# Attention and a gated feed-forward layer on one core: whole steps of 512 columns in place of half steps in the first two blocks

## The chip, the core and the metric

The kernel runs on one core of a Trainium2 chip. The core has five engines with queues of their own, each of which works its instructions in the order in which they were issued: PE (TensorE, matrix products, results in the accumulator memory PSUM), DVE (VectorE) and ACT (ScalarE) for element-wise work, POOL (GpSimd, used for constants only) and SP (SyncE, which here issues all transfers). An engine whose next instruction waits for another engine does nothing else meanwhile. The metric is the device time of one execution in microseconds; the time before is the median of three runs.

## What is computed

A chunked local attention with eight memory keys per head, followed by a feed-forward layer of two products with a piecewise gate between them. Batch 4, 8 heads, 768 tokens, head size 64: 3072 tokens of width 512, hidden width 2048, all in 32-bit floats.

```python
for c in range(nc):                      # 24 chunks of 32 tokens
    l_start, r_end = max(0, c_start - 16), min(S, c_end + 8)
    k_full = np.concatenate([mem_k, k[:, :, l_start:r_end]], axis=2)
    v_full = np.concatenate([mem_v, v[:, :, l_start:r_end]], axis=2)
    scores = scale * np.matmul(q_c, k_full.transpose(0, 1, 3, 2))
    scores = scores - np.max(scores, axis=-1, keepdims=True)
    a = np.exp(scores)
    a = a / (np.sum(a, axis=-1, keepdims=True) + 1e-09)
    out[:, :, c_start:c_end] = np.matmul(a, v_full)
...
h = x @ w_in
g = np.where(h >= 1, h, np.where(h <= -1, 0.0, (h + 1) ** 2 / 4))
return g @ w_out
```

## The kernel before

The 3072 tokens are six blocks of 512 (`TB`), each of two halves of 256 (`HT`). The hidden width is 16 slices of 128 (`fc`). A **step** is one block and one slice: the hidden product (the slice of `w_in` against the block's x, giving 128 hidden values for the block's tokens), the gate, and the output product, which adds into four PSUM banks that hold the block's output until the slice 15 is in.

To keep the precision, x, weights and gate are each split into a high and a low part that PE takes, and each product is the sum of three: high by high, low by high, high by low. A whole step is so 12 hidden matmuls with 512 moving columns (tokens) and 12 output matmuls (four tiles of 128 tokens by three kinds) with 512 moving columns (output features). A half step is 12 hidden matmuls with 256 columns and 6 output matmuls with 512.

The gate of a step is three ACT operations (two Relu from PSUM into `gw` and `gt`, a Square), a sum on DVE (`gw`), a cast on ACT that makes the high part (`gh`), and a subtraction on DVE that makes the low part (`gl`). In the loop these are `gating`, `gate_sum`, `gate_high` and `gate_low` (lines 420 to 444), for half steps the same is written out in `half_step` (457 to 501).

The weights come as 64-bit words, 16 tensors of 1 MB, each with two slices. `decode` (153 to 173) makes them into high and low parts: a scaling on ACT, a shift and two combinations on DVE (`f`), a cast on ACT (`hi`, tile `wr`), a subtraction on DVE (`lo`, tile `wr`). All operations are 1024 columns wide. `weight_order` (614 to 619) says which slices come first: tensor 0 holds the hidden slices 0 and 1, tensor i the hidden slice i + 1 and the output slice i - 1.

The attention of block 0 is done in four pieces, g0 and g1 for its first half and g2 and g3 for its second (`first_attention`, 217 to 287), so that x of the first half is ready early. Each has 13 stages: scores on PE, maximum, subtraction, exponential (ACT), four operations of normalising on DVE, a transpose on PE, a copy on ACT, the values product on PE, and x's high (ACT) and low part (DVE). Those of the later halves, n0, n1 and so on (`attention`, 374 to 387), have transposes on DVE and 18 stages.

Up to the end of block 1 the order of issue is written out by hand, in the string `FIRST` (32 to 55). Each word there advances one chain by one stage, and everything that the stage has is issued at that place on the queue of its engine. `g` and `n` are attention pieces, `w` the decoding of a weight tensor, `+` the next load on SP's queue (the list `early`, 526 to 533). `A` and `B` are the half steps of block 0's first and second half, `C` and `D` those of block 1: `A7` is the first half with slice 7. A half step has six stages: hidden product; the three ACT operations; sum; high part; low part; output product. The last slice has two more, in which the results are copied and stored. Two consecutive half steps share one set of gate tiles. Hidden products use two PSUM banks in turn (`ps_h`); outputs have the four banks `a0` and `a1`; scores and values of the attention use the two banks `s`. The PSUM tiles of g0 to g3 lie in `s`, `a0` and `a1` (`PLACES`, 215).

From block 2 on a loop (570 to 605) issues whole steps: in each the hidden product of step s and the output product of step s - 2, with pieces of the next attention between. In its first two rounds, where there is no step s - 2 of its own, it finishes the last `LAST` = 4 half steps, two in a round.

Every operation is recorded through one helper, so the profile gives nearly all of them the line 68; they are told apart by tile: `ps_h` are hidden products, `ps_o` output products, `ps_s` scores, `ps_x` values, `f` and `wr` decoding, `gw`, `gt`, `gh` and `gl` gates, `xth` and `xtl` x, `mx`, `pr`, `den`, `rin` and `pt` attention, `ob` stored results.

Of the kernel before, what the change touches and what calls it, by code (L numbers as in the profile page):

```python
# [16 lines left out]
P = 128  # L17
CHUNK, LEFT, RIGHT = 32, 16, 8
TB = 512
# [18 lines left out]
    w10 + A4 B3 w5 B4 A5 w11 w6 + B4 w6 A4 w7 w7 B4 A5 B5 B4 w12 + A5 w6 B4 A5 B5 A5 w7 w13 A6 + B5  # L38
    w7 w8 A5 w8 B5 A6 B6 B5 w14 A6 w7 A6 B5 B6 A6 w8 w15 A7 B6 w8 w9 A6 w9 B6 A7 B6 B7 A7 w8 A7 B6
    B7 A7 w9 A8 B7 w9 w10 w10 A7 B7 A8 B7 B8 A8 w9 A8 B7 A8 B8 w10 A9 B8 w10 w11 w11 B8 A8 A9 B8 A9  # L40
    B9 w10 A9 A9 B8 w11 B9 B9 A10 w11 w12 w12 B9 A9 A10 B9 w11 B10 A10 w12 A10 B9 B10 A10 w12 w13
    A11 B10 w13 B10 A10 A11 B10 w12 n0 A11 w13 A11 B11 + n0 w13 B10 A11 B11 n0 A12 B11 n0 w13 B11
    A11 A12 n0 B12 n0 n0 B11 n0 B11 B12 A12 n0 A12 A13 A12 n0 n0 A12 A13 w14 n0 B13 w14 n0 A14 B13
    n0 B12 n0 w14 B12 B12 w14 A13 w15 B12 A13 + w14 n0 A13 A14 B14 w15 A13 n0 n0 B14 B13 n1 w15 B13
    B13 w15 A15 A14 + n1 A14 B13 A15 A14 w15 B15 n1 A14 B14 n1 A15 B14 n1 C0 A15 B15 n1 n1 B14 n1
    B14 C0 A15 n1 A15 n1 n1 C1 n1 n1 C2 C1 B15 n1 B15 C0 B15 n1 C0 A15 C2 C0 C1 A15 C2 C1 C2 B15 C1
    + n1 C2 n1 n1 C0 B15 D0 B15 C1 D0 D0 D1 D0 D0 C3 D1 D1 C2 D1 C3 D1 D0 C3 C3 C3 D2 D1 D2 D2 D3 D2
    D2 C4 D3 D3 C3 D3 C4 D3 D2 C4 C4 C4 D4 D3 D4 D4 D5 D4 D4 C5 D5 D5 C4 D5 C5 D5 D4 C5 C5 C5 D6 D5
    D6 D6 C6 D6 D6 D7 C6 C6 C5 D7 C6 D7 D6 C6 D7 D7 C7 n2 C7 C7 D8 C7 + n2 C6 n2 D8 D8 D7 n2 C7 D8
    n2 C8 D8 n2 n2 D9 C8 n2 C7 n2 D9 n2 n2 D8 C8 n2 C8 C9 D9 n2 D9 C8 D10 n2 C9 D9 C9 C8 D10 C9 D10  # L50
    D9 C9 D10 D10 n2 C10 + n2 n2 n2 D11 C10 C10 n3 D11 C10 D11 C10 C9 D11 + n3 D10 n3 C11 D11 n3 n3
    D12 C11 n3 n3 C10 n3 D12 n3 D11 n3 n3 C12 C11 n3 C11 D12 D13 C12 C11 n3 D12 n3 C11 D13 D12 C12
# [21 lines left out]
def attn_ffn_kernel(ctx: ExitStack, tc: tile.TileContext, first_qk, first_v, qk, vw, w, out):  # L74
# [380 lines left out]
    items = []  # L455

    def half_step(blk, half, fc):

        n = len(items)
        items.append((blk, half, fc))  # L460
        q = slice(half * HT, (half + 1) * HT)
        xh, xl = (x[:, :, q] for x in xts[blk])
# [33 lines left out]
        ob = apool.tile([P, 2, DM], F32, name="ob", tag="f", bufs=2)  # L496
        for t, copy in enumerate((dve.tensor_copy, act.copy)):
            copy(ob[:, t], acc[blk][2 * half + t])
            r0 = blk * TB + (2 * half + t) * P
            sp.dma_start(out[r0 : r0 + P, :], ob[:, t])  # L500
            yield
# [199 lines left out]
```

## Time and profile before

| | us |
|---|---|
| median of 3 runs (lowest, highest) | 614.69 (614.47, 614.77) |
| the profiled execution | 613.78 |
| its span, from the first to the last instruction | 612.0 |
| PE busy | 594.5 (97%), 5784 matmuls |
| DVE busy | 330.8 (54%) |
| ACT busy | 291.1 (48%) |
| moved by transfers | 55.36 MB |

The times of rows in the profile count from the span's start. In a row of the order of time, start and length in us come first, then the engine, the operation, what it writes and reads, shapes and the number of instructions merged; in brackets stands the idle time of the engine just before and what ended it. A matmul's recorded length has its way through the array in it, so that consecutive ones overlap: what one costs is read from start to start. "x" is a number of instructions. The granted clock of PE is a share of its full one.

### The profile page before, as it was taken

Reading aid. Unit: us, or ns where it says so; the run is one execution under the profiler, and the core shown is the slowest. Engines: PE = TensorE matmul, PEld = TensorE weight load, DVE = VectorE, ACT = ScalarE, POOL = GpSimd, SP = SyncE. Lnnn points to the kernel's source line nnn. Section 1 sums busy time; section 2 is a strip of 40 time slices with the busy share of each in tenths; the row PEclk is TensorE's granted clock in tenths of the full one; section 3 lists DMA queues with packets and bytes.
Section 4 is the critical chain, followed back from the end, with each engine's and each line's share of the span. In section 5 each row is a group of like instructions: output and inputs, shape, how many; then the busy total and the mean of one; then the engine's idle time right before and its main releaser. Section 6 shows DMA issues by size and latency. Waiting matters only on the chain.

```text
span 612.0 us, 12987 instructions
## 1 busy us (share of the span) xinstructions
PE 594.5 (97%) x5784; PEld 498.4 (81%) x5784; DVE 330.8 (54%) x514; ACT 291.1 (48%) x599; POOL 0.7 (0%) x6
## 2 busy tenths in 40 slices
PE   5799999999999999999999999999999999999996
PEld 3789998889988988888887888888888888888885
DVE  5899999983276734635523644722563632322222
ACT  3689865555444553444344343434443444433442
POOL 0000000000000000000000000000000000000000
PEclk8699999999999999999999999999999999999999
DMA  8999002422023213122201222100410000100001
GB/s 357 423 417 412 9 1 105 140 79 96 1 104 114 76 56 112 61 71 104 71 0 70 104 70 105 60 11 16 158 70 2 0 2 0 70 0 2 0 1 69
DMA packets 9848, 55.36 MB, mean 90 GB/s; under 512 B 1088, under 2 KB 1088, under 8 KB 5184
## 3 DMA queue, kind: packets, MB, share of 16 engines
q1 hardware_dynamic: 9792, 54.53, 23.4%
q8 instruction: 45, 0.74, 0.5%
q14 instruction: 11, 0.09, 0.0%
HBM read 48.23 MB, written 6.29 MB: 89 GB/s over the span
## 4 chain that ended last, share of the span: by engine, by line
PE 78%; DVE 18%; issue 2%; DMA 1%; ACT 1%; DVEq 0%; ACTq 0%
PE ps_o L68 37%; PE ps_h L68 36%; DVE f L68 7%; PE ps_x L68 3%; DVE wr L68 3%; PE ps_s L68 2%; DVE gw L68 2%; DVE pr L68 2%; DVE gl L68 1%; DVE pt L68 1%; DVE mx L68 1%; DVE den L68 1%; DMA qk<-in_first_qk_dram 1%; DVE xtl L68 0%; ACT pr L68 0%
## 5 line engine op out<-in xcount | busy, mean ns | idle before, releaser
L68 PE MATMUL ps_h<-xth,wr 128*128 128x256 f32 (+1 forms) x1024 | 202.9, 340 | 0.3 <-ACT xth L68 0.3
L68 PE MATMUL ps_o<-wr,gh 128*128 128x512 f32 x768 | 202.6, 395 | 0.5 <-DVE wr L68 0.5
L68 PEld LDWEIGHTS ps_h<-xth,wr 128*128 128x128 f32 x1024 | 164.4, 190 | 26.9 <-ACT xth L68 0.6
L68 PEld LDWEIGHTS ps_o<-wr,gh 128*128 128x128 f32 x768 | 141.3, 188 | 30.4 <-DVE wr L68 0.9
L68 DVE SCALAR_TENSOR_TENSOR gw<-gw,gt 128x256 f32<-128x256 f32 (+1 forms) x128 | 71.0, 556 | 167.3 <-ACT gw L68 166.5
L68 ACT ACTIVATE gw<-ps_h 128x256 f32<-128x256 f32 (+1 forms) x128 | 62.7, 490 | 161.2 <-PE ps_h L68 159.5
L68 PE MATMUL ps_o<-wr,gl 128*128 128x512 f32 x384 | 112.8, 395 | 0.2 <-DVE gl L68 0.2
L68 PE MATMUL ps_h<-xtl,wr 128*128 128x256 f32 (+1 forms) x512 | 110.4, 337 | 0.1
L68 DVE TENSOR_TENSOR gl<-gw,gh 128x256 fp32r<-128x256 f32 (+1 forms) x128 | 70.9, 555 | 66.5 <-ACT gh L68 65.7
L68 ACT CAST gh<-gw 128x256 fp32r<-128x256 f32 (+1 forms) x128 | 65.5, 514 | 65.3 <-DVE gw L68 65.2
L68 PEld LDWEIGHTS ps_h<-xtl,wr 128*128 128x128 f32 x512 | 83.6, 190 | 10.5 <-DVE xtl L68 0.3
L68 PEld LDWEIGHTS ps_o<-wr,gl 128*128 128x128 f32 x384 | 72.4, 189 | 17.5 <-DVE gl L68 0.6
L68 ACT ACTIVATE gw<-gw 128x256 f32<-128x256 f32 (+1 forms) x128 | 67.4, 526 | 0.0
L68 ACT ACTIVATE gt<-ps_h 128x256 f32<-128x256 f32 (+1 forms) x128 | 62.2, 486 | 0.0
L68 DVE STREAM_TRANSPOSE pt<-pr 32x512 f32<-32x512 f32 (+1 forms) x60 | 41.2, 698 | 1.3
L68 DVE SCALAR_TENSOR_TENSOR f<-w,f 128x1024 uint32<-128x1024 uint32 x32 | 39.1, 1221 | 0.4
L68 ACT ACTIVATE pr<-pr 128x1024 f32<-128x1024 f32 (+1 forms) x14 | 13.1, 937 | 41.0 <-DVE pr L68 41.0
L68 PEld LDWEIGHTS ps_x<-pt,v 64*64 64x64 f32 x1536 | 25.7, 142 | 5.8 <-issue 3.4
L68 PE MATMUL ps_x<-pt,v 64*64 64x32 f32 x1536 | 27.6, 226 | 1.5 <-DVE pt L68 0.9
L68 ACT CAST xth<-ps_x 128x512 fp32r<-128x512 f32 x24 | 13.0, 590 | 24.7 <-PE ps_x L68 24.7
L68 PEld LDWEIGHTS ps_s<-qk 64*32 64x32 f32 x1536 | 16.6, 108 | 8.2 <-issue 4.6
L68 PE MATMUL ps_s<-qk 64*32 64x64 f32 x1536 | 19.3, 232 | 3.6 <-issue 1.4
(27 smaller groups left out, 179.3 us busy)
## 6 DMA issues: line engine op xcount, KB each, us to landing
w<-in_w_dram SPq DMA_DIRECT2D x16, 1024.0 KB, 19.8
qk<-in_qk_dram SPq DMA_DIRECT2D x10, 1536.0 KB, 6.7
v<-in_vw_dram SPq DMA_DIRECT2D x10, 1024.0 KB, 4.9
out_dram<-ob SPq DMA_DIRECT2D x24, 256.0 KB, 2.0
qk<-in_first_qk_dram SPq DMA_DIRECT2D x4, 768.0 KB, 8.7
v<-in_first_v_dram SPq DMA_DIRECT2D x4, 512.0 KB, 12.8
```

Source lines behind the costliest of these rows:

```text
L68: return self.tc.keep_in_program_order(getattr(self.engine, name)(*args, **kwargs))
```

## The change

`half_step` becomes `early_step`, which takes the tiles of 128 tokens that it shall work on: two of them (256 tokens, as before) or all four (512). With four, the hidden product has 512 columns, the gate's operations are 512 wide and have their own set of tiles, and the output product has 12 matmuls. New letters stand for whole steps in the order of issue: `J` for block 0, `E` for block 1. Only the slices 0 to 3 of both blocks stay halves (A0 to A3, B0 to B3, C0 to C3, D0 to D3); J4 to J15 and E4 to E15 are whole. `FIRST` is a new list of 496 words instead of 638. The four half steps that the loop finished are now two whole ones (`LAST` = 2), which is the same work.

The new list also has another order in the parts that stay the same: g2's scores come before g1's and g0's values, the first two pieces of g2's softmax stand inside w0's decoding, three hidden products (A0, A1, A2) precede g3's transposes, n0's scores come between B2's hidden and A2's output product, n0's other stages are spread over w9 to w14.

```diff
-LAST = 4
+LAST = 2
...
-    def half_step(blk, half, fc):
-
-        n = len(items)
-        items.append((blk, half, fc))
-        q = slice(half * HT, (half + 1) * HT)
-        xh, xl = (x[:, :, q] for x in xts[blk])
-        hp = ps_h.tile([P, 512], F32, name="ps_h")[:, 0:HT]
+    items, halves = [], []
+
+    def early_step(name, blk, tokens, fc):
+
+        items.append(name)
+        size = len(tokens) * P
+        xh, xl = (x[:, :, tokens[0] * P : tokens[0] * P + size] for x in xts[blk])
+        n = 0
+        if size < TB:
+            n = len(halves) % 2
+            halves.append(name)
+        hp = ps_h.tile([P, 512], F32, name="ps_h")[:, 0:size]
...
-        g, t, gh, gl = (x[:, n % 2 * HT : (n % 2 + 1) * HT] for x in both["g"])
+        g, t, gh, gl = (x[:, n * HT : n * HT + size] for x in tiles)
...
-        pe_products(acc[blk][2 * half : 2 * half + 2], gh, gl, wh, wl, fc)
+        pe_products([acc[blk][t] for t in tokens], gh, gl, wh, wl, fc)
...
+    parts = {"A": (0, (0, 1)), "B": (0, (2, 3)), "J": (0, range(NT))}
+    parts |= {"C": (1, (0, 1)), "D": (1, (2, 3)), "E": (1, range(NT))}
...
-            for blk, half, fc in items[len(items) - LAST :][i * n : (i + 1) * n]:
-                for _ in chains[f"{'ABCD'[2 * blk + half]}{fc}"]:
+            for name in items[len(items) - LAST :][i * n : (i + 1) * n]:
+                for _ in chains[name]:
```

The two lists, up to the place where J4 begins and the matching place of the old one (line breaks of the file):

```diff
-    + + g0 g0 g0 + g0 g1 g0 + g0 g0 g1 g1 g0 g1 + g1 g0 w0 g1 g1 + g1 g0 w0 g1 w0 + g0 g1 w0 w0 g2 +
-    g0 w0 g1 w1 g2 + g2 g1 g0 g3 g2 + g1 g2 A0 + g3 g3 g2 g2 g3 g2 A1 A0 + g3 w2 g3 g3 g3 g2 w1 A1
-    w1 + g2 g3 w3 w1 g2 g3 A0 w1 g3 w2 + w2 g2 g3 A0 g2 w4 g3 A0 B0 w1 + w2 A0 B0 A1 w2 B0 B1 w3 +
-    B0 w2 A1 A2 B1 B0 A1 w3 A1 + A2 B1 w5 w3 B0 B1 A2 w3 + B1 B2 w4 A2 w3 w6 B1 A2 B2 + w4 A3 w7 B2
-    w4 B2 A2 A3 + B2 w5 w4 B3 A3 w5 w8 B2 A3 w4 + B3 A4 w9 A3 B3 w5 B3 A3 + A4 B3 w6 w5 A4 B4 w6 A4
+    + + g0 g0 + g0 g1 g0 + g0 g1 g1 g0 g0 + g1 g0 w0 g1 g0 + g1 g1 g1 g0 w0 g1 + w0 g2 g1 w0 g1 g2 +
+    w0 g2 w1 g0 w0 + g2 w1 g1 g2 + g0 g2 g2 g2 + g0 g2 w1 g3 g2 g1 w1 + A0 w2 g3 w1 g3 A1 w2 + g3 w1
+    w3 g3 g2 A0 g3 g3 + A1 g3 A2 w2 g2 w4 g3 g2 A2 A0 w2 g3 A0 + g3 w3 w2 A0 w3 A0 g3 g3 + w2 B0 A1
+    w3 A3 A1 B0 + A1 w3 B0 B1 w4 B0 w3 A3 A1 + B1 B0 w4 w5 B2 B1 w6 A2 w4 n0 + A2 B1 A2 w4 B1 A2 A3
+    w5 A3 B2 + A3 w5 B3 w8 B2 w7 B0 w4 + B2 w5 B3 A3 w9 B2 B3 B1 w6 B3 + w5 w6 J4 w10 B3 w5 + w6 w11
```

More of the change, by code (lines that the diff above doesn't have):

```diff
@@ L38 @@
[L38 to L52, printed above, removed]
@@ new lines @@
+    J12 n0 J13 w13 J12 J14 + n0 w14 n0 n0 w14 J12 w14 J14 J13 J14 w15 J14 n1 w15 w15 J15 + n1 w15
+    w15 J13 J15 n1 J15 n1 J14 C0 J15 n1 J14 n1 n1 C0 n1 n1 J15 C1 n1 n1 J15 n1 C1 n1 n1 C1 C0 C1 C2
+    J15 J15 C0 C1 n1 J15 J15 C0 C2 C2 C0 + n1 C2 n1 n1 C3 C2 C1 C3 C3 D0 C3 C3 C2 D0 D0 D1 D0 D0 n2
+    D1 D1 D2 D1 + n2 C3 D1 D2 n2 D0 D2 n2 D2 D3 n2 D2 D1 n2 n2 D3 n2 E4 D3 n2 D3 n2 n2 n2 D2 E4 D3
+    n2 E5 n2 E4 E4 E4 D3 E5 E6 E5 E5 E5 E4 E6 E6 E6 n2 E6 E7 + n2 n2 n2 n3 E7 E5 + n3 n3 E7 E8 n3 E7
@@ L468, in half_step @@
         yield
-        if n % 2 == 0:
-            both["g"] = (
+        if n == 0:
+            tiles = (
                 gpool.tile([P, TB], F32, name="gw", tag="gw"),
@@ L475, in half_step @@
             )
-        g, t, gh, gl = (x[:, n % 2 * HT : (n % 2 + 1) * HT] for x in both["g"])
+            if size < TB:
+                both["g"] = tiles
+        else:
+            tiles = both["g"]
+        g, t, gh, gl = (x[:, n * HT : n * HT + size] for x in tiles)
         act.activation(g, hp, AF.Relu, bias=0.5, scale=0.5)
@@ L488, in half_step @@
             acc.setdefault(blk, [None] * NT)
-            pair = two_banks(f"a{half}", "ps_o")
-            acc[blk][2 * half : 2 * half + 2] = [pair[:, t] for t in range(2)]
+            pair = two_banks(f"a{tokens[0] // 2}", "ps_o")
+            for t in tokens:
+                acc[blk][t] = pair[:, t % 2]
         wh, wl = weights(1, fc, 0), weights(1, fc, 1)
-        pe_products(acc[blk][2 * half : 2 * half + 2], gh, gl, wh, wl, fc)
+        pe_products([acc[blk][t] for t in tokens], gh, gl, wh, wl, fc)
         yield
@@ L495, in half_step @@
             return
[L496 to L500, printed above, removed]
+        for t in tokens:
+            if t % 2 == 0:
+                ob = apool.tile([P, 2, DM], F32, name="ob", tag="f", bufs=2)
+            (act.copy if t % 2 else dve.tensor_copy)(ob[:, t % 2], acc[blk][t])
+            r0 = blk * TB + t * P
+            sp.dma_start(out[r0 : r0 + P, :], ob[:, t % 2])
             yield
```

17 lines of the change are left out of this document (9 added, 8 removed).

## Prediction

> **What bounds the kernel now.** I read the page first, then six stretches of the trace cut where the PE's behaviour changes, then the order of time of PE, DVE and ACT inside them. The page's chain of work that ended last:
>
> ```profile
> PE 78%; DVE 18%; issue 2%; DMA 1%; ACT 1%; DVEq 0%; ACTq 0%
> ```
>
> The chain runs through DVE first and PE later. The table by stretch says where the hand-over is (columns: PE, PE weight load, DVE, ACT, POOL busy us with instruction counts, granted PE clock, DMA share, GB/s):
>
> ```profile
> 0.00:22.86 22.86, 13.72 (x400) 9.48 (x401) 14.03 (x24) 8.58 (x11) 0.70 (x6) 0.75 0.93 376
> 22.86:36.27 13.41, 11.18 (x180) 9.48 (x180) 12.99 (x21) 9.77 (x19) 0.00 (x0) 0.92 1.02 424
> 36.27:92.76 56.49, 56.49 (x361) 51.06 (x360) 56.28 (x85) 47.19 (x103) 0.00 (x0) 1.00 0.45 186
> 92.76:140.00 47.24, 45.74 (x751) 40.82 (x751) 43.49 (x71) 24.90 (x64) 0.00 (x0) 1.00 0.35 121
> 140.00:223.40 83.40, 83.40 (x1003) 75.58 (x1002) 43.73 (x85) 40.34 (x115) 0.00 (x0) 1.00 0.21 73
> 223.40:612.00 388.60, 383.94 (x3098) 312.00 (x3096) 160.27 (x232) 160.28 (x288) 0.00 (x0) 1.00 0.13 48
> ```
>
> From 36.27 us on PE is never idle except for 1.5 us between 92.76 and 140 (47.24 less 45.74) and the stores at the very end. DVE is just as full from 36.27 to 92.76 (56.28 of 56.49): decoding of weights, gates and the first attention all sit in its queue. So the first 140 us are a tie of two full engines, and from 140 us on it is PE alone (DVE busy 43.73 of 83.40). The issue list that the change rewrites ends at 223.40, where the loop's first whole step starts; all after that has the same instructions in both kernels. The end therefore moves by three things: the pure PE work of the list, PE time lost before the unbroken stretch, and PE gaps after it.
>
> **Part 1: PE work of whole steps.** The unbroken stretch 36.27 to 92.76 holds 360 matmuls: 20 half hidden products of 12 and 20 half output products of 6. That is 56.49 / 20 = 2.825 us for a half step, 5.65 for two halves. In the loop a whole step is read from two starts, three steps apart:
>
> ```profile
> 303.19 2.01 PE L68 MATMUL ps_h<-xth,wr 128*128 128x512 f32 x8
> 319.85 2.01 PE L68 MATMUL ps_h<-xth,wr 128*128 128x512 f32 x8
> ```
>
> 16.66 / 3 = 5.55 us. A pair of halves made into one whole step saves 5.65 - 5.55 = 0.096 us (24 matmuls of 256 columns become 12 of 512; the 12 output matmuls stay the same). The change makes whole steps of 12 pairs in each of two blocks: 24 x 0.096 = 2.3 us. In block 1 nothing else competes, so its half of this is safe. [...]
>
> **Part 2: relief of DVE and ACT.** The gates by both widths, and the decoding that shares their queues:
>
> ```profile
> L68 DVE TENSOR_TENSOR gl<-gw,gh 128x512 fp32r<-128x512 f32 x64 | 44.3, 693 | 60.1 <-ACT gh L68 60.1
> L68 DVE SCALAR_TENSOR_TENSOR gw<-gw,gt 128x512 f32<-128x512 f32 x64 | 44.2, 691 | 138.2 <-ACT gw L68 137.8
> L68 DVE SCALAR_TENSOR_TENSOR f<-w,f 128x1024 uint32<-128x1024 uint32 x32 | 39.1, 1221 | 0.4
> L68 ACT ACTIVATE gw<-gw 128x512 f32<-128x512 f32 x64 | 40.5, 632 | 0.0
> L68 ACT CAST gh<-gw 128x512 fp32r<-128x512 f32 x64 | 39.8, 622 | 41.7 <-DVE gw L68 41.7
> L68 ACT ACTIVATE gw<-ps_h 128x512 f32<-128x512 f32 x64 | 38.1, 595 | 127.7 <-PE ps_h L68 127.7
> L68 ACT ACTIVATE gt<-ps_h 128x512 f32<-128x512 f32 x64 | 37.9, 593 | 0.0
> L68 ACT ACTIVATE gw<-gw 128x256 f32<-128x256 f32 x64 | 26.9, 420 | 0.0
> L68 DVE SCALAR_TENSOR_TENSOR gw<-gw,gt 128x256 f32<-128x256 f32 x64 | 26.7, 422 | 29.1 <-ACT gw L68 28.6
> L68 DVE TENSOR_TENSOR gl<-gw,gh 128x256 fp32r<-128x256 f32 x64 | 26.5, 418 | 6.3 <-ACT gh L68 5.6
> L68 ACT CAST gh<-gw 128x256 fp32r<-128x256 f32 x64 | 25.6, 407 | 23.6 <-DVE gw L68 23.5
> L68 ACT ACTIVATE gw<-ps_h 128x256 f32<-128x256 f32 x64 | 24.6, 384 | 33.5 <-PE ps_h L68 31.9 <-DVE gl L68 1.3 <-issue 0.3
> L68 ACT ACTIVATE gt<-ps_h 128x256 f32<-128x256 f32 x64 | 24.3, 380 | 0.0
> L68 ACT ACTIVATE w<-w 128x1024 f32<-128x1024 f32 x16 | 18.8, 1176 | 0.0
> ```
>
> A whole step costs DVE 691 + 693 = 1.38 us against 2 x (422 + 418) = 1.68, so 0.30 less; ACT 595 + 593 + 632 + 622 = 2.44 against 2 x (384 + 380 + 420 + 407) = 3.18, so 0.74 less. For the 12 pairs of block 0 that is 3.6 us of DVE work out of a full queue, 8.9 of ACT. By itself this buys no time where PE is full too; it buys back PE's gaps where PE waited for DVE, which are these:
>
> ```profile
> 109.14 0.30 PE L68 MATMUL ps_x<-pt,v 64*64 64x32 f32 x4 [0.31 <-DVE pt L68]
> 109.88 1.94 PE L68 MATMUL ps_x<-pt,v 64*64 64x32 f32 x116 [0.43 <-DVE pt L68]
> 116.60 1.47 PE L68 MATMUL ps_s<-qk 64*32 64x64 f32 x128 [0.36 <-issue]
> 127.39 0.50 PE L68 MATMUL ps_o<-wr,gl 128*128 128x512 f32 x1 [0.20 <-DVE gl L68]
> 132.00 1.94 PE L68 MATMUL ps_x<-pt,v 64*64 64x32 f32 x116 [0.20 <-DVE pt L68]
> ```
>
> 0.31 + 0.43 + 0.36 + 0.20 + 0.20 = 1.5 us. Whether they go depends on the new order. For each list I added up the work queued on DVE up to the last transpose of an attention, and on PE up to the values product that reads it. DVE's work is counted by starts, which lie about 0.09 us closer than the durations (1.13 us for a 1024-wide operation, 0.60 for 512, 0.33 for 256); PE's by 1.43 and 1.39 us for the half products, 2.75 and 2.78 for the whole ones. For n0 DVE stands 8.9 us behind PE in the old list (96.6 against 87.7) and 7.8 in the new one (91.7 against 83.9); for n1 8.6 and 7.4. DVE comes 1.1 to 1.2 us earlier relative to PE. I take back 1.1 of the 1.5; the ends are 0 and 1.5.
>
> **Part 3: the start.** The rows that matter, DVE, then PE:
>
> ```profile
> 17.71 1.23 DVE L68 TENSOR_TENSOR wr<-f,wr 128x1024 fp32r<-128x1024 f32 x1 [1.17 <-ACT wr L68]
> 22.97 0.69 DVE L68 TENSOR_REDUCE mx<-ps_s 128x8 f32<-128x512 f32 x1 [0.92 <-PE ps_s L68]
> 37.50 1.22 DVE L68 TENSOR_TENSOR wr<-f,wr 128x1024 fp32r<-128x1024 f32 x1
> ```
> ```profile
> 22.86 2.07 PE L68 MATMUL ps_h<-xth,wr 128*128 128x256 f32 x8
> 24.73 0.77 PE L68 MATMUL ps_h<-xtl,wr 128*128 128x256 f32 x4
> 30.46 1.14 PE L68 MATMUL ps_x<-pt,v 64*64 64x32 f32 x64 [0.40 <-ACT pt L68]
> 36.27 1.11 PE L68 MATMUL ps_h<-xth,wr 128*128 128x256 f32 x8
> 37.69 1.12 PE L68 MATMUL ps_h<-xth,wr 128*128 128x256 f32 x8
> ```
>
> The old list makes DVE wait 1.17 us for ACT in w0's decoding and 0.92 for g3's scores. The new one puts g2's maximum and subtraction into the first wait and moves g3's behind w1's decoding, so both are filled. I count DVE's new queue from w0's last operation at 17.71 to w2's last one: eight 1024-wide operations (9.0 us), thirteen 512-wide (7.9), four small ones (0.8), two 256-wide (0.7): 18.5 us, so w2 is ready near 36.4 to 36.9 (the later end for operations that wait for the one before). In the old list it is ready at 37.50 + 1.14 = 38.6.
>
> PE's side: the new list queues hidden products of A0, A1, A2, then g3's transposes and values, A0's output, B0's hidden, and then A3's hidden, which needs w2. g3's values stand behind a long ACT queue: after g3's exponential (done near 27.2 by the same count) come, by starts that on ACT lie about 0.11 us closer than durations, two scalings of weights (1.05 each), three gates of three operations (0.85 each), g2's cast (0.5) and the copy itself (0.6), 5.8 us, so PE gets them near 33 and idles some 2.8 us before that. By 36.9 it has then done five half products. The old kernel has five at 37.69 (A0, A1, B0 hidden, A0 out, B1 hidden). Gain 0.8 us. Its ends: 2.2 us, if PE follows DVE's lead fully; and a loss of 1, if one of these hand-overs slips.
>
> The lead must hold afterwards. In the old list the furthest that a needed DVE result stands behind PE in these sums is 10.0 (A0's output), in the new one 11.3 (outputs of A2 and A3) and 11.2 (J4's output); DVE's head start of about 2 us pays for the 1.3. From J5 on no lag is over 10.2.
>
> **The rest, at nothing.** n0's scores move from behind B10 to behind B2's hidden: the same 1.5 us of PE, and the key buffer is free 50 us earlier, for a load that the idle DMA (0.45 and 0.35 of its time in these stretches) hides. SP's queue still issues the same 34 transfers, block 0's four stores among them. The two whole steps left to the loop hold what four halves held. Were any of this cover gone, one whole product would cost 2.75 us once.
>
> **Sum.** 2.3 + 1.1 + 0.8 = 4.2 us. The profiled execution took 613.78 us (span 612.0 and 1.78 around it), 0.91 under the median of 614.69; taken off the span the result is 607.8, off the profiled time 609.6, off the median 610.5, which is my number. A measurement here tells about 0.2% (1.2 us) from no change, so 613.5 and 615.9 bound "same".
>
> **Rivals.**
>
> *Only the pace arrives.* The lead at the start is lost in PE's new 2.8 us hole, and PE's gaps near 110 to 133 us move instead of closing. Against it stand the filled DVE waits. For it: the hole sits in front of work that starts at a low clock today; the eight matmuls at 22.86 take 1.87 us to the next row, where eight at the pace of the twelve from 36.27 to 37.69 take 0.95 (granted clock 0.75 in the first stretch, 0.92 in the second). If the hole brings that back, up to a dozen matmuls lose 0.11 us each, 1.3 us, more than the 0.8. [...] Time: 614.7 - 2.3 = 612.4.
>
> *DVE's queue blocks on whole gates.* Slower. A gate of 512 columns takes from PE's last product to its low part about 1.6 (ACT, three operations by starts) + 0.69 + 0.62 + 0.69 = 3.6 us, a half 0.85 + 0.42 + 0.41 + 0.42 = 2.1. DVE works its list strictly in order, so where a whole gate's sum or low part comes to the head of the queue before ACT has finished, the decoding behind it (w5 to w15) waits, and PE waits for the weights. The place is J4 to J15, 12 steps. DVE's relief pays for 0.30 us a step; beyond that PE slips. With w us of waiting a step the result is 614.7 - 2.3 - 0.8 + (12 w - 3.6), so it is slower than before from w = 0.56; at 0.75, half of the extra latency, it gives 617.0. Against it: DVE's waits from 36.27 to 140 in the old kernel are small though its list is as dense,
>
> ```profile
> DVE gw L68 <- ACT gw L68: 1.5, 1, 1.5
> DVE xtl L68 <- ACT xth L68: 0.5, 1, 0.5
> DVE den L68 <- ACT pr L68: 0.5, 1, 0.5
> DVE gl L68 <- ACT gh L68: 0.4, 1, 0.4
> ```
>
> and in the new list four other products, over 8 us of PE, stand between a whole step's hidden product and its output, against the gate's 3.6.
>
> *The change moves work but no end.* If block 0 stays bound by DVE and the new order loses at the start what block 1 gains (12 x 0.096 = 1.2 us), the time is 613.5 to 615.9, say 614.5.
>
> **Chances.** Forecast 0.55 (609.0 to 611.9); only the pace 0.23 (611.9 to 613.5); no end moved 0.10; blocked DVE 0.12. Faster 0.78, same 0.10, slower 0.12. The range leaves out the blocked case, some half of "same", and a small chance of all upper ends together (2.3 + 1.5 + 2.2 = 6.0): 608.7 to 614.3.
>
> **What would show it.** In the new profile: the list should end (first 512-wide hidden product after E15's) near 219 instead of 223.4; starts of whole steps 5.55 us apart from J6 on; DVE's waits at 17.7 and 23 gone and w2 ready near 36.5; a PE hole of about 3 us before g3's values near 33; PE idle under 0.5 us between 92 and 140. The forecast is wrong if DVE waits for ACT at the gates by over 0.3 us a step, if PE idles after 37 us, or if the granted clock falls near 33.

## The result and the profile after

The changed kernel takes 608.10 us (median of four runs, 607.99 to 608.29) against 614.58 for the old one (four runs, 613.84 to 614.77): a ratio of 0.9887, with a 95% interval of 0.986 to 0.9913. It is 6.5 us faster where 4.2 were forecast, and 0.6 us under the lower end of the forecast range. The profiled executions lie 5.6 us apart: 608.17 with a span of 606.4 after, against 613.78 and 612.0.

The page of the changed kernel, its chain of work that ended last:

```profile
PE 94%; DVE 3%; ACT 1%; DMA 1%; issue 0%; DVEq 0%; ACTq 0%
```

DVE carried 18% of this chain before and 3% now: after the start, nothing but PE sets the end. The table by stretch of the changed kernel, cut at the first hidden product, at the hidden product that needs w2 (36.77; its counterpart in the old kernel starts at 37.69, one half product behind the old table's cut at 36.27), at 92, at 140 and at the first whole step of block 2 (columns as before):

```profile
0.00:23.72 23.72, 14.56 (x404) 10.17 (x404) 16.60 (x30) 9.00 (x12) 0.70 (x6) 0.69 0.94 378
23.72:36.77 13.05, 11.47 (x192) 10.75 (x187) 12.91 (x20) 10.07 (x19) 0.00 (x0) 0.90 1.01 419
36.77:92.00 55.23, 55.23 (x386) 46.13 (x385) 54.87 (x70) 45.52 (x75) 0.00 (x0) 1.00 0.52 216
92.00:140.00 48.00, 47.98 (x641) 40.53 (x642) 41.92 (x61) 23.22 (x49) 0.00 (x0) 1.00 0.28 100
140.00:217.76 77.76, 77.76 (x801) 64.16 (x796) 39.14 (x58) 33.95 (x66) 0.00 (x0) 1.00 0.19 69
217.76:606.40 388.64, 383.99 (x3097) 312.00 (x3095) 160.12 (x231) 159.43 (x285) 0.00 (x0) 1.00 0.13 48
```

The list ends at 217.76 instead of 223.40, 5.64 us earlier, and the rest takes 388.64 instead of 388.60: the whole gain lies in the list, and none of it is given back later. Between 92 and 140 PE is idle for 0.02 us. From 36.77 on the granted clock is 1.00, and PE stops for nothing longer until the stores at the end.

The order of time on PE in the changed kernel, at the five places of the forecast:

```profile
21.59 1.08 PE L63 MATMUL ps_h<-ident,pr 128*128 128x128 f32 x4 [1.76 <-DVE pr L63]
22.61 1.19 PE L63 MATMUL ps_s<-qk 64*32 64x64 f32 x64
23.72 2.08 PE L63 MATMUL ps_h<-xth,wr 128*128 128x256 f32 x8
...
32.77 1.14 PE L63 MATMUL ps_x<-pt,v 64*64 64x32 f32 x64 [1.58 <-ACT pt L63]
...
36.77 1.12 PE L63 MATMUL ps_h<-xth,wr 128*128 128x256 f32 x8
...
103.85 2.07 PE L63 MATMUL ps_x<-pt,v 64*64 64x32 f32 x128
105.85 2.40 PE L63 MATMUL ps_h<-xth,wr 128*128 128x512 f32 x8
...
109.01 2.03 PE L63 MATMUL ps_o<-wr,gh 128*128 128x512 f32 x8
...
128.91 2.07 PE L63 MATMUL ps_x<-pt,v 64*64 64x32 f32 x128
130.91 1.19 PE L63 MATMUL ps_o<-wr,gh 128*128 128x512 f32 x4
...
195.55 2.01 PE L63 MATMUL ps_h<-xth,wr 128*128 128x512 f32 x8
...
201.10 2.01 PE L63 MATMUL ps_h<-xth,wr 128*128 128x512 f32 x8
```

Whole steps start 5.55 us apart (195.55 to 201.10). Products of the attention values, 128 small matmuls, take 2.00 us from start to start, both n0's (103.85 to 105.85) and n1's (128.91 to 130.91). The hole in front of g3's values is 1.58 us long and the clock stays up behind it (1.00 from 32.77 to 36.77). The same places in the old kernel, with what the prediction did not quote:

```profile
108.52 0.32 PE L68 MATMUL ps_x<-pt,v 64*64 64x32 f32 x8
...
111.75 1.20 PE L68 MATMUL ps_o<-wr,gh 128*128 128x512 f32 x4
...
125.17 1.09 PE L68 MATMUL ps_o<-wr,gh 128*128 128x512 f32 x4
...
128.42 1.11 PE L68 MATMUL ps_h<-xth,wr 128*128 128x256 f32 x8
...
131.38 0.42 PE L68 MATMUL ps_x<-pt,v 64*64 64x32 f32 x12
...
133.87 0.73 PE L68 MATMUL ps_o<-wr,gh 128*128 128x512 f32 x2
```

n0's values took 3.23 us there (108.52 to 111.75), n1's 2.49 (131.38 to 133.87): 1.23 and 0.49 more than now. The brackets of these products in the old trace show only 0.74 and 0.20 of idle time.

DVE's start in the changed kernel, and its waits between 37 and 140 us:

```profile
16.54 0.68 DVE L63 TENSOR_REDUCE mx<-ps_s 128x8 f32<-128x512 f32 x1
17.26 0.69 DVE L63 TENSOR_TENSOR pr<-ps_s,mx 128x512 f32<-128x512 f32 x1
17.87 1.22 DVE L63 TENSOR_TENSOR wr<-f,wr 128x1024 fp32r<-128x1024 f32 x1
...
35.54 1.21 DVE L63 TENSOR_TENSOR wr<-f,wr 128x1024 fp32r<-128x1024 f32 x1
```
```profile
DVE gw L63 <- ACT gw L63: 3.0, 3, 1.5
DVE gl L63 <- ACT gh L63: 0.9, 2, 0.5
```

The maximum and subtraction of g2 stand where DVE waited 1.17 us, w0's last operation starts at 17.87 with no wait, and w2's last one at 35.54 instead of 37.50. At the gates DVE waits 3.9 us in all, 0.33 a step if all of it is put on the 12 whole steps; this costs PE nothing, since PE is not idle there.

### The profile page after: what moved, and what is told of

It reads as the page before. It is cut to its first block, busy times and chain, and to the rows that moved or that the text cites. A ratio compares the mean times of both kernels' runs of the same rounds, so it can differ in the third digit from the quotient of the medians.

```text
span 606.4 us, 12265 instructions
## 1 busy us (share of the span) xinstructions
PE 591.0 (97%) x5496; PEld 483.7 (80%) x5496; DVE 325.6 (54%) x466; ACT 281.2 (46%) x503; POOL 0.7 (0%) x6
## 4 chain that ended last, share of the span: by engine, by line
PE 94%; DVE 3%; ACT 1%; DMA 1%; issue 0%; DVEq 0%; ACTq 0%
PE ps_o L63 44%; PE ps_h L63 44%; PE ps_x L63 3%; PE ps_s L63 3%; DVE f L63 1%; DMA qk<-in_first_qk_dram 1%; DVE pr L63 1%; DVE mx L63 0%; DVE den L63 0%; ACT w L63 0%; ACT gw L63 0%; DVE wr L63 0%; DVE xtl L63 0%; ACT pr L63 0%; ACT wr L63 0%
## 5 line engine op out<-in xcount | busy, mean ns | idle before, releaser
L63 PE MATMUL ps_h<-xth,wr 128*128 128x512 f32 (+1 forms) x832 | 197.3, 379 | 0.0
L63 PEld LDWEIGHTS ps_h<-xth,wr 128*128 128x128 f32 x832 | 148.7, 189 | 31.9 <-DVE wr L63 0.5
L63 DVE SCALAR_TENSOR_TENSOR gw<-gw,gt 128x512 f32<-128x512 f32 (+1 forms) x104 | 67.2, 648 | 170.0 <-ACT gw L63 169.5
L63 ACT ACTIVATE gw<-ps_h 128x512 f32<-128x512 f32 (+1 forms) x104 | 58.7, 564 | 167.8 <-PE ps_h L63 167.7
L63 PE MATMUL ps_h<-xtl,wr 128*128 128x512 f32 (+1 forms) x416 | 105.2, 375 | 0.0
L63 DVE TENSOR_TENSOR gl<-gw,gh 128x512 fp32r<-128x512 f32 (+1 forms) x104 | 67.4, 649 | 67.4 <-ACT gh L63 67.3
L63 ACT CAST gh<-gw 128x512 fp32r<-128x512 f32 (+1 forms) x104 | 61.1, 590 | 68.7 <-DVE gw L63 68.7
L63 ACT ACTIVATE gw<-gw 128x512 f32<-128x512 f32 (+1 forms) x104 | 62.5, 601 | 0.0
L63 ACT ACTIVATE gt<-ps_h 128x512 f32<-128x512 f32 (+1 forms) x104 | 58.2, 559 | 0.0
L63 ACT CAST wr<-f 128x1024 fp32r<-128x1024 f32 x16 | 16.8, 1050 | 9.3 <-DVE f L63 9.3
```

What stands on the lines that cost most here:

```text
L63: return self.tc.keep_in_program_order(getattr(self.engine, name)(*args, **kwargs))
```

## The experiments

The theory after the result: the 5.6 us are 2.3 of pace, 0.9 at the start and some 2.2 around n0 and n1. Its rivals: the last term comes from the order alone, or from the width's relief of DVE alone; or the start's part is not DVE's wait.

**e5: block 1 by halves again.** The changed kernel with each E written as C and D at the same place; block 0 as changed.

```diff
...
-    n2 E5 n2 E4 E4 E4 D3 E5 E6 E5 E5 E5 E4 E6 E6 E6 n2 E6 E7 + n2 n2 n2 n3 E7 E5 + n3 n3 E7 E8 n3 E7
+    D4 D3 n2 C5 D5 n2 C4 D4 C4 D4 C4 D4 D3 C5 D5 C6 D6 C5 D5 C5 D5 C5 D5 C4 D4 C6 D6 C6 D6 C6 D6 n2
...
-LAST = 2
+LAST = 4
```

> The new kernel with block 1's whole steps issued as two halves, one behind the other at the same places; start and block 0 as in the new kernel. The pace of 12 pairs, seen from the other side than in the run on block 1 with the old list. Theory (0.096 us a pair): 608.1 + 1.15 = 609.3. If PE stalls inside a run of matmuls without waiting for another engine, as it did for 1.1 us in block 1 of the run with halves at the new places, up to 1.4 more, 610.7. [...]

609.72 us (609.72 to 610.03), ratio to the old kernel 0.9914 (0.9889 to 0.994). Its span is 607.9, 1.5 over the changed kernel's. PE has a stop of 0.38 us at 29.07 that no engine causes, but this costs nothing: the hole before g3's values is 1.25 us instead of 1.58, and the product that needs w2 starts at 36.81 against 36.77. So the pace is best read inside block 1. From the first hidden product of slice 4 to the loop's first whole step it takes 70.97 us here (148.06 to 219.03) and 69.65 in the changed kernel (148.11 to 217.76): 1.3 us, or 0.11 a pair. By PE's last matmul (602.55 against 601.35) the difference is 1.2. The pace is confirmed by its size, and is if anything a little over the forecast's 0.096.

**e1: only block 1 whole, in the old order.** The old list, in which C and D from slice 4 on become E at the later of their two places.

```diff
-    D2 C4 D3 D3 C3 D3 C4 D3 D2 C4 C4 C4 D4 D3 D4 D4 D5 D4 D4 C5 D5 D5 C4 D5 C5 D5 D4 C5 C5 C5 D6 D5
+    D2 D3 D3 C3 D3 D3 D2 E4 D3 E4 E4 E4 E4 E5 E5 E4 E5 E5 E5 E6 E6 E6 E5 E6 E6 E7 n2 E7 E7 E7 + n2
...
-LAST = 4
+LAST = 2
```

> The old list of issue, only block 1's slices 4 to 15 as whole steps (each stage of a whole step stands where the later of its two halves stood); block 0 and the start are as before. It prices the pace alone, where nothing but PE is full. If a pair of halves costs 0.096 us more than a whole step (the theory): 12 x 0.096 = 1.15 us less, 613.4 against 614.6, and in the profile a span of 610.9 against 612.0. [...] If block 1 also lost time that the profile doesn't show as idle: 2 us or more.

614.98 us (614.13 to 615.58), ratio 1.0008 (1.0 to 1.0017): the expected 1.2 us did not appear. The merged list has a new gap on PE,

```profile
206.28 2.12 PE L66 MATMUL ps_o<-wr,gh 128*128 128x512 f32 x8 [1.38 <-ACT gh L66]
```

an output product placed too close behind its whole gate. Two more things in this profile have nothing to do with block 1. The stop of PE at the start is 1.67 us, where the old kernel's profile has 1.05 (below), and the row at 36.27 there starts at 37.12 here. And behind n0's values, whose idle pieces are those of the old kernel (0.33 and 0.43 us here, 0.31 and 0.43 there), the granted clock falls to 0.50:

```profile
112.62 1.81 PE L66 MATMUL ps_o<-wr,gh 128*128 128x512 f32 x4
117.09 1.08 PE L66 MATMUL ps_o<-wr,gh 128*128 128x512 f32 x4
```
```profile
114.00:116.00 2.00, 2.00 (x9) 1.72 (x8) 2.00 (x3) 1.51 (x5) 0.00 (x0) 0.50 0.86 311
```

Six outputs and a half hidden product take 4.47 us from start to start here; the same work took 2.93 in the old kernel (111.75 to 114.68). PE so comes to n1's scores 2.0 us later (118.57 against 116.60), and the outputs around n1 lose nothing any more (1.48 us for the six, 2.79 for the twelve), although DVE's work up to there is unchanged: a later PE closes these gaps as well. As a measure of the pace this run is inconclusive; its new gap shows that a whole gate without room in front of its output product costs as much as the pace gives in block 1.

**e3: the new order, all steps by halves.** The changed list with each J and E split into its two halves in place.

```diff
...
-    B2 w7 J4 w7 J5 + w6 w7 w12 w6 + w7 B3 J4 J5 w8 J6 w7 + J4 J5 w13 J4 w9 J5 J4 J6 w9 + J5 w15 J6
+    w11 B2 w7 A4 B4 w7 A5 B5 + w6 w7 w12 w6 + w7 B3 A4 B4 A5 B5 w8 A6 B6 w7 + A4 B4 A5 B5 w13 A4 B4
...
-LAST = 2
+LAST = 4
```

> The new list with every whole step issued as its two halves, one right after the other at the same places: order without width. Theory: the start gains 0.9 us as in the new kernel, the pace nothing, and with 0.30 us more DVE work a step the gaps at n0 and n1 are back: 614.6 - 0.9 = 613.7. Rival (the order closes the gaps): 614.6 - 0.9 - 2.0 = 611.7.

612.77 us (612.45 to 613.11), ratio 0.9973 (0.9962 to 0.9983), between the two expectations. Its span of 610.7 has a stop of PE of 1.10 us at 172.67 that no engine causes; 609.6 without it. PE's waits from 92 to 140 are one:

```profile
PE ps_h L68 <- DVE wr L68: 0.7, 1, 0.7
```

So the new order by itself closes most of the gaps. n0's values take 2.00 us (104.87 to 106.87) and n1's 1.99 (130.70 to 132.69), as in the changed kernel. What is left stands behind n0's values, where PE waits for weights:

```profile
106.87 0.73 PE L68 MATMUL ps_h<-xth,wr 128*128 128x256 f32 x4
109.31 1.12 PE L68 MATMUL ps_h<-xth,wr 128*128 128x256 f32 x8
```

This half hidden product takes 2.44 us where an undisturbed one takes 1.43, and some 0.1 more goes in the outputs behind it: 1.1 us lost in all. The old kernel lost 2.7 around n0 and n1 and the changed one loses 0.5 (both counted below), so the order brings 1.6 and the width 0.6. The spans agree: old 612.0, less 0.9 for the start is 611.1; e3's 609.6 leaves 1.5 to the order; the further 3.2 down to 606.4 are 2.3 to 2.6 of pace and 0.6 to 0.9 of width. This split rests on single profiles, and by the spans on taking the stop off.

**e2: whole steps in the old order.** Both blocks merged as in e1.

```diff
...
-    w10 + A4 B3 w5 B4 A5 w11 w6 + B4 w6 A4 w7 w7 B4 A5 B5 B4 w12 + A5 w6 B4 A5 B5 A5 w7 w13 A6 + B5
+    J4 w11 w6 + J4 w6 w7 w7 J4 J5 J4 w12 + w6 J4 J5 w7 w13 + J5 w7 w8 w8 J5 J6 J5 w14 w7 J5 J6 w8
...
-LAST = 4
+LAST = 2
```

> The old list in both blocks, whole steps for the slices 4 to 15 (each stage where the later of its halves stood). Width without the new order. Theory: the pace gives 2.3 us, and DVE's relief of 0.30 us a step closes the gaps of PE around n0 and n1 (about 2 us lost there by starts, 1.5 of it idle); the start is unchanged: 614.6 - 4.3 = 610.3. Rival: the gaps are closed by the new places of n0 and n1, not by width; then the pace alone is left, 612.3, and the gaps near 110 to 133 us are still in the profile. Second rival: stages set at the later place come too late and open new gaps; then over 612.3.

623.63 us (617.95 to 623.97), ratio 1.0129 (1.01 to 1.0158): slower than either expectation, by the mechanism of the second rival, new gaps. The order of time on PE at n0's values, and the table by stretch behind it:

```profile
109.00 0.30 PE L63 MATMUL ps_x<-pt,v 64*64 64x32 f32 x4 [1.68 <-DVE pt L63]
109.74 2.71 PE L63 MATMUL ps_x<-pt,v 64*64 64x32 f32 x116 [0.43 <-DVE pt L63]
112.39 3.78 PE L63 MATMUL ps_o<-wr,gh 128*128 128x512 f32 x8
```
```profile
106.00:112.00 6.00, 3.72 (x127) 3.03 (x127) 5.84 (x8) 2.64 (x5) 0.00 (x0) 0.88 0.01 3
112.00:117.00 5.00, 5.00 (x27) 3.97 (x22) 5.00 (x8) 1.59 (x3) 0.00 (x0) 0.50 0.61 210
```

PE reaches n0's values before DVE has their transposes, 2.3 us of idle time in pieces; then the granted clock falls to 0.50, and eight output matmuls take 3.78 us where the changed kernel's take 2.03. At a second place PE stops for 2.53 us without a releaser (at 201.75), and eight output matmuls behind it take 3.17, the clock being 0.50 again from 203 to 206. The executions of this run differ by 6 us (617.95 to 623.97), and the profile is of the longest. The run changes two things at once, the width and, by the rule of the later place, where each stage stands. It shows that whole steps merged so into the old order cost more than they give; it does not price the width's relief alone.

**e10: the new order with DVE's relief taken back.** The changed kernel with one 256-wide operation more on DVE in each whole gate of block 0 (12 x 0.33 = 4.0 us).

```diff
         dve.scalar_tensor_tensor(g, g, 1.0, t, op0=ALU.min, op1=ALU.add)
+        if blk == 0 and size == TB:
+            dve.tensor_tensor(spare, spare, spare, op=ALU.subtract)
...
+    spare = const.tile([P, HT], F32, name="spare")
+    pool.memset(spare, 0.0)
```

> The new kernel with one more DVE operation of 256 columns before each gate's low part in the 12 whole steps of block 0 (0.33 us each by starts, 4.0 us in all: what two half gates would cost more than a whole one). Width's relief of DVE taken back, pace and order kept. If the relief is what closed the gaps around n0 and n1: up to 2 us, 610. If the order closed them: DVE waits 4.4 us between 37 and 140 in the new kernel, which take the work up, and the time is 608.1 to 608.6.

612.97 us (611.84 to 613.52), ratio 0.9961 (0.9943 to 0.9979), 4.9 us slower than the changed kernel and well past what either expected. PE at the same place, and its stretch:

```profile
104.72 1.94 PE L63 MATMUL ps_x<-pt,v 64*64 64x32 f32 x116 [0.43 <-DVE pt L63]
107.05 2.07 PE L63 MATMUL ps_h<-xth,wr 128*128 128x512 f32 x4 [0.40 <-ACT wr L63]
110.12 2.08 PE L63 MATMUL ps_h<-xth,wr 128*128 128x512 f32 x4 [1.00 <-DVE wr L63]
```
```profile
108.00:112.00 4.00, 3.00 (x8) 1.84 (x7) 4.00 (x5) 1.25 (x4) 0.00 (x0) 0.50 0.65 252
```

1.8 us of idle time: n0's values break up again (0.43), and the larger waits are for the weights of the hidden product behind them (0.40 and 1.00). And again a clock of 0.50: this hidden product takes 5.6 us without its 1.00 of waiting (107.05 to 113.69), where the changed kernel's takes 3.2 (105.85 to 109.01). So about half of the 4.9 us is the clock. n1's values take 2.00 us (133.57 to 135.57), with PE 4.7 us later there than in the changed kernel.

What this run takes back is also more than what the width gives. By starts, as the prediction counts DVE's queue, the operations of two half gates take 4 x 0.33 = 1.32 us and those of a whole one 2 x 0.60 = 1.20: a relief of 0.12 us a step, 1.4 in the 12 steps, against the 4.0 put back here. So the run shows how little room DVE has at n0 even in the new order; it does not show that the relief of 1.4 us was needed. For that e3 is the measure: without width 1.1 us are lost there, with it 0.5.

**e6 and e9: less work for DVE in the old kernel.** The third operation of decoding is left out for the tensors 5 to 9 (e6) and 5 to 15 (e9, with `if i < 5`): these weights lose their signs.

```diff
-        dve.scalar_tensor_tensor(f, u, 0x80000000, f, op0=ALU.bitwise_and, op1=ALU.bitwise_or)
+        if i not in range(5, 10):
+            dve.scalar_tensor_tensor(f, u, 0x80000000, f, op0=ALU.bitwise_and, op1=ALU.bitwise_or)
```

> The kernel before, with the decoding of the tensors 5 to 9 shortened by its third DVE operation (the signs of these weights are left out): 5 x 1.13 = 5.7 us less work in DVE's queue between 50 and 90 us, everything else as before. If DVE's full queue makes the gaps of PE around n0 and n1: the lost 2 us between 92 and 140 go, 614.5 - 2.0 = 612.5, and the stretch before 92 does not change, because PE is full there. If the gaps come from the places of n0 and n1 in PE's queue or from accumulator banks: 614.5.

> The kernel before, with the third DVE operation of the decoding left out for all tensors from 5 to 15 (the signs of these weights are left out): 11 x 1.13 = 12.4 us less in DVE's queue, 7 of it while n0 and n1 are worked on. With five tensors n0's loss went from 1.23 to 0.35 us and n1's (1.5 us in three places) stayed. If n1's losses are DVE's load too: PE's lost time between 92 and 140 us falls from 2.4 to about 1.1, what the new kernel has there, and the time to 612.0. If they come from n1's place (13.4 us of PE products between its scores and its values for a softmax chain of nearly that length; 15.4 in the new list): they stay, 613.2.

e6: 613.32 us (612.86 to 613.97), ratio 0.9975 (0.9962 to 0.9989). e9: 612.76 (612.08 to 616.51), ratio 0.9959 (0.9935 to 0.9982). Both lie between their expectations. PE at n0's values, first in e6, then in e9:

```profile
108.63 2.42 PE L68 MATMUL ps_x<-pt,v 64*64 64x32 f32 x128
110.98 1.19 PE L68 MATMUL ps_o<-wr,gh 128*128 128x512 f32 x4
```
```profile
109.33 2.26 PE L68 MATMUL ps_x<-pt,v 64*64 64x32 f32 x128
111.52 1.21 PE L68 MATMUL ps_o<-wr,gh 128*128 128x512 f32 x4
```

From start to start 2.35 and 2.19 us, where the old kernel has 3.23 and the changed one 2.00: DVE's load was the cause at n0. The six outputs before n1's scores take 1.94 us in e6 (113.89 to 115.83; 1.92 in the old kernel) and 1.49 in e9 (114.44 to 115.93), which also lightens DVE's later decoding: this loss was DVE's load too. The idle piece there has no releaser in the profile, but a row of DVE explains it. In the old kernel

```profile
115.21 1.28 DVE L68 TENSOR_TENSOR xtl<-ps_x,xth 128x512 fp32r<-128x512 f32 x2
```

is the last read of n0's values out of the banks `s`, into which n1's scores go. It ends at 116.49, and the scores start at 116.60; in e6 the pair is 115.72 and 115.83. The twelve outputs take 3.25 us in e6 as in the old kernel and 2.80 in e9. n1's values stay slow in both: 2.47 us in e6 and 2.39 in e9 (130.26 to 132.65), so this part, 0.4 us, is not shown to be DVE's load. In all the losses around n0 and n1 are 1.8 us in e6 and 0.7 in e9, of the old kernel's 2.7. e9's profile is of an execution of 615.04 us, over the run's median: it has a stop of 2.27 us at 196.75, behind the places read here.

**e4: the wait at the start put back.** The changed kernel with g2's maximum and subtraction behind w0's last operation.

```diff
-    + + g0 g0 + g0 g1 g0 + g0 g1 g1 g0 g0 + g1 g0 w0 g1 g0 + g1 g1 g1 g0 w0 g1 + w0 g2 g1 w0 g1 g2 +
-    w0 g2 w1 g0 w0 + g2 w1 g1 g2 + g0 g2 g2 g2 + g0 g2 w1 g3 g2 g1 w1 + A0 w2 g3 w1 g3 A1 w2 + g3 w1
+    + + g0 g0 + g0 g1 g0 + g0 g1 g1 g0 g0 + g1 g0 w0 g1 g0 + g1 g1 g1 g0 w0 g1 + w0 g2 g1 w0 g1 + w0
+    w1 g0 w0 g2 g2 + g2 w1 g1 g2 + g0 g2 g2 g2 + g0 g2 w1 g3 g2 g1 w1 + A0 w2 g3 w1 g3 A1 w2 + g3 w1
```

> The new kernel with g2's maximum and subtraction put back behind w0's last DVE operation, so that DVE waits for ACT in w0's decoding again (1.17 us before). One change of order in the start, undone. Theory: DVE's queue sets the start, so w2 and the first unbroken stretch of PE come 1.0 to 1.2 us later, and the time is 609.2 against 608.1. Rival: the hole of 1.6 us that PE has before g3's values takes the delay up, and the time stays at 608.1.

609.52 us (609.29 to 609.6), ratio 0.9919 (0.9906 to 0.9932), as the theory had it. DVE's row, then the product on PE that needs w2:

```profile
17.48 1.22 DVE L63 TENSOR_TENSOR wr<-f,wr 128x1024 fp32r<-128x1024 f32 x1 [1.17 <-ACT wr L63]
```
```profile
37.80 1.12 PE L63 MATMUL ps_h<-xth,wr 128*128 128x256 f32 x8
```

The 1.17 us of waiting are back, the product moves from 36.77 to 37.80, and the span from 606.4 to 607.5. Here a wait in DVE's full queue is passed on to the end.

**e7: the same wait filled in the old kernel.**

```diff
-    + + g0 g0 g0 + g0 g1 g0 + g0 g0 g1 g1 g0 g1 + g1 g0 w0 g1 g1 + g1 g0 w0 g1 w0 + g0 g1 w0 w0 g2 +
-    g0 w0 g1 w1 g2 + g2 g1 g0 g3 g2 + g1 g2 A0 + g3 g3 g2 g2 g3 g2 A1 A0 + g3 w2 g3 g3 g3 g2 w1 A1
+    + + g0 g0 g0 + g0 g1 g0 + g0 g0 g1 g1 g0 g1 + g1 g0 w0 g1 g1 + g1 g0 w0 g1 g2 w0 + g0 g1 w0 g2
+    g2 w0 + g0 w0 g1 w1 + g1 g0 g3 g2 + g1 g2 A0 + g3 g3 g2 g2 g3 g2 A1 A0 + g3 w2 g3 g3 g3 g2 w1 A1
```

> The old list with one change in the start: g2's scores move ahead of g0's values and g2's maximum and subtraction into DVE's first wait, before w0's last operation, as in the new list; g3's maximum stays where it was. If the filled wait is what the start gained by: 614.5 - 1.2 = 613.3. Rival: PE stops inside g3's scores, at its 350th matmul, in every run of the old start (1.05 to 2.03 us, no other engine awaited) and never in the new one; if that stop comes from the supply of instructions, g3's scores end at the same 23 us, DVE waits longer for them, and the time stays within 0.4 of 614.5.

614.72 us (613.85 to 618.01), ratio 1.0003 (0.9985 to 1.0021): no gain; the rival's number. PE in the scores of g3:

```profile
19.94 0.45 PE L68 MATMUL ps_s<-qk 64*32 64x64 f32 x13
22.05 1.06 PE L68 MATMUL ps_s<-qk 64*32 64x64 f32 x51 [1.66 <-issue]
```

The 0.88 us for which PE waited for DVE there (0.45 us of scores started at 20.36 in the old kernel) are gone, but PE then stops for 1.66 us in the middle of one product with nothing to wait for; the old kernel stops there for 1.05. DVE, which needs these scores, waits 1.17 us for them instead. So in the old order filling DVE's wait alone gains nothing: the stop, 0.6 us longer here, takes it up.

**e11: the stop moved.** The stop comes at PE's 350th matmul. In the old kernel the 8 warming matmuls of 512 columns become 68 of 60 columns, so that every later instruction of PE stands 60 places further back in the stream.

```diff
-            pe.matmul(ps, warm[:, 0:P], warm, start=True, stop=True)
+            pe.matmul(ps[:, 0:60], warm[:, 0:P], warm[:, 0:60], start=True, stop=True)
...
-    keep_warm(8)
+    keep_warm(68)
```

> The kernel before, with its 8 warming matmuls of 512 columns made 68 of 60 columns (about the same time): every later matmul stands 60 places further in PE's stream. If PE's stop of 1.05 to 2.03 us at its 350th matmul comes from the supply of instructions, it stays near the 350th and so moves out of g3's scores into g1's values product; if it has to do with g3's scores themselves, it stays at their 14th matmul, now the 410th. The time is not forecast to a microsecond: 614.5, within 1.5.

The stop is again at the 350th matmul, which now lies in g1's values, 60 matmuls earlier in the work:

```profile
17.78 0.74 PE L68 MATMUL ps_x<-pt,v 64*64 64x32 f32 x17
20.10 1.50 PE L68 MATMUL ps_x<-pt,v 64*64 64x32 f32 x47 [1.58 <-issue]
```

So in these two kernels it goes with a place in PE's instruction stream, not with the work. The time, 620.08 us (619.09 to 621.59), ratio 1.0079 (1.0055 to 1.0103), was not as expected: more such stops appeared, of 2.9 us at 34.50 and 2.6 at 124.44, and the granted clock is 0.50 behind them (36 to 40 and 126 to 128 us); behind the first, eight hidden matmuls of 256 columns take 2.19 us from start to start (35.17 to 37.36), where the changed kernel's at 36.77 take 0.96.

**e8: a try at the hole before g3's values.** The changed kernel with g3's copy ahead of w4's scaling and of A2's gate, g3's x earlier, and A3's and B1's hidden products exchanged.

```diff
-    w3 g3 g2 A0 g3 g3 + A1 g3 A2 w2 g2 w4 g3 g2 A2 A0 w2 g3 A0 + g3 w3 w2 A0 w3 A0 g3 g3 + w2 B0 A1
-    w3 A3 A1 B0 + A1 w3 B0 B1 w4 B0 w3 A3 A1 + B1 B0 w4 w5 B2 B1 w6 A2 w4 n0 + A2 B1 A2 w4 B1 A2 A3
+    w3 g3 g2 A0 g3 g3 + A1 g3 A2 w2 g2 g3 g3 w4 g2 A2 A0 w2 A0 + g3 g3 w3 w2 A0 g3 w3 A0 + w2 B0 A1
+    w3 B1 A1 B0 + A1 w3 B0 A3 w4 B0 w3 B1 A1 + A3 B0 w4 w5 B2 B1 w6 A2 w4 n0 + A2 B1 A2 w4 B1 A2 A3
```

> The new kernel with PE's hole before g3's values (1.58 us) made smaller: ACT copies g3's transposed probabilities ahead of w4's scaling and A2's gate, g3's x parts go ahead of w2's cast and of w3's first combination, and the hidden products of A3 and B1 change places, since B1 does not need w2. If PE from the first hidden product on is what ends last (the chain of the new kernel is 94% PE): 0.8 us less, 607.3. If DVE's queue (w2 ready at 36.7) still sets the pace behind it: PE stalls later by as much and the time stays at 608.1.

608.88 us (608.6 to 609.91), ratio 0.9902 (0.9878 to 0.9925): 0.8 slower than the changed kernel. The hole of 1.58 becomes one of 0.68, and a new one of 1.07 opens behind it:

```profile
33.90 1.19 PE L63 MATMUL ps_o<-wr,gh 128*128 128x512 f32 x4 [1.07 <-ACT gh L63]
```

The product that needs w2 starts at 36.81, against 36.77. The hole was slack of PE against the queues of DVE and ACT, not lost time. That the run is slower fits the next product, which waits 0.29 us for ACT and starts 0.5 us later (38.71 against 38.21); the span is 0.6 longer.

## Why the prediction was right in its direction and too small

**Pace, 2.3 us: right, a little small.** Whole steps are 5.55 us apart, and e5 puts 1.2 to 1.3 us on block 1's 12 pairs, where the forecast has 1.15. For all 24 pairs that makes an estimated 2.4 to 2.6.

**Start, 0.8 us: right.** The product that needs w2 starts at 36.77 against 37.69, so 0.92. The queue counts held: w2's last operation ends 1.13 us after 35.54, at 36.7, in the forecast's 36.4 to 36.9. The hole was forecast at 2.8 us and is 1.58, at 32.77 as said. e4 shows DVE's wait as the cause in the changed kernel, and in e5 and e8, where PE's hole is smaller, the product starts at 36.81 all the same. What the step did not see is the stop of PE that sat behind the same rows of the old kernel: filling the wait alone gained nothing there (e7).

**Gaps around n0 and n1, "I take back 1.1 of the 1.5; the ends are 0 and 1.5": the step that failed, a mis-sized term.** That they close was right, with PE idle for 0.02 us. But the term was a sum of idle brackets, and a product that runs in pieces loses more than the brackets show. From start to start the old kernel lost 1.23 us in n0's values, 0.49 in n1's, 0.53 in the six outputs before n1's scores (114.68 to 116.60 in the old trace, 1.92 where the forecast's own pace for six is 1.39), and 0.47 in the twelve outputs from 125.17 to 128.42 (3.25 against 2.78): 2.7 us. The changed kernel still loses 0.5 behind n0 (105.85 to 109.01 is 3.16 against 2.76 for a whole hidden product, and 0.1 in the outputs behind it). 2.2 us came back, twice the term and above its upper end. With it and the pace as measured the sum is 5.5 to 5.7, and the list became 5.6 shorter. That DVE was late is shown by e6 and e9 for n0's values and for the outputs around n1, not for n1's values (0.4 us). The new order brings 1.6 of the 2.2 even without width (e3), and the width 0.6; both are read from single profiles. Whether the width does its part by relieving DVE or ACT, or by the whole product itself, no run separates.

The same part counts DVE's relief as 0.30 us a step and 3.6 in all, from durations, though it counts DVE's queue by starts. By starts it is 0.12 and 1.4. The 1.1 was made from starts and does not have this slip; the price of the rival on blocked gates, 0.30 us a step to pay with, has it.

**The base, "off the median 610.5": the second step that failed.** The sum was made on a profiled execution 0.8 to 0.9 us under its kernel's median and then taken off the median; off the profiled time it gave 609.6. The changed kernel's profiled execution lies at its median (608.17 and 608.10). The other 0.8 to 0.9 us of the 6.5 are therefore a part of the old kernel's usual time that its profile has less of. It is this part that took the result out of the range: off the median the 5.6 us alone give 609.1, inside 608.7 to 614.3.

Where the old kernel usually loses it stays open, for no execution near its median has a profile. The stop at the start is one candidate: 1.05 us in the old kernel's profile, but 1.67, 1.67 and 2.03 in those of e1, e9 and e2, which share that start (0.96 in e6). A longer stop is passed on: the row that starts at 36.27 in the old kernel starts at 37.12, 37.07 and 37.50 in these (36.38 in e6). In the changed kernel PE has just waited 1.76 us for DVE at 21.59, and the next scores, 64 at 22.61, run through. The clock behind n0's values is another: it stayed at 1.00 in the old kernel's profile and fell to 0.50 in e1's with nearly the same idle pieces, which took 1.5 us. Both are argued, not shown: no run varied either alone.

**The rivals.** *Only the pace*: no, start and gaps came, and the granted clock did not fall near 33 (1.00 from 32.77 to 36.77). *DVE blocks on whole gates*: in the changed kernel DVE waits up to 0.33 us a step, slightly over the 0.3 that the forecast set as a sign against it, and yet none of it reaches PE: as a sign it was set too low. In the old order the whole gates did make the kernel slower (e2), through n0's transposes, the clock behind them and a stop, not by a wait at each gate: between 37 and 140 us DVE waits for a gate once, for 4.7 us, behind that place. *No end moved*: no.

## What to carry to other kernels

Count what a gap costs from start to start against an undisturbed product of the same kind; the idle brackets are its lower end (0.74 us of brackets in n0's values, made of 128 small matmuls, where 1.23 were lost). Count a full engine's queue by starts too, its relief included: by durations DVE's relief came out at 3.6 us, by starts at 1.4. With PE and DVE both full up to 92 us, width and order were worth most together: the order alone gave under a third of the gain (e3), and the width merged into the old order a loss (e2). And see where the profiled execution lies among the runs before taking a difference off the median.

## What was not expected of the hardware

**PE can stop with nothing to wait for that the profile shows.** In the profiles with the old start PE stops for 0.96 (e6) to 2.03 us (e2) at its 350th matmul, in a run of small matmuls; with 60 matmuls more ahead of it, the stop keeps its index, 1.58 us long (e11). The longest stop of this kind is 2.89 us, at 34.50 in e11. The old kernel's page has a queue of instruction transfers,

```profile
q8 instruction: 45, 0.74, 0.5%
```

about 16 KB each (0.74 MB in 45), and the stretch up to there has the DMA engines busy for 0.93 of the time. That PE waits for such a transfer is the author's guess: no row names one, and no run varied the transfers.

**The clock can fall behind short idle pieces.** In e2 the granted clock was 0.50 from 112 to 117 us and in e10 from 108 to 112, after idle pieces of at most 1.68 us (2.3 in sum) and at most 1.00 (1.8 in sum) around a product of small matmuls. In e1 two pieces of 0.33 and 0.43 us came before a clock of 0.50 (114 to 116), while behind the old kernel's 0.31 and 0.43 at the same place, and behind the changed kernel's single hole of 1.58, it stayed at 1.00. What the condition is, these runs don't settle. The price is known: some 1.5 us in e1 and 2.5 in e10 beside the idle time itself.
